# A dense squared-ReLU layer: block 0 starts its first matmuls on half the columns, with the other transposes in between

## Chip, cores, metric

One core of a Trainium2 chip. The metric is the device time of one launch in microseconds, as a median of runs. The program runs on one core, so a run has no second die to be compared with; every run quoted here was fast (within 1.5% of the fastest run of the same kernel). A profile is one execution, taken with the hardware profiler; its span is about 1.8 us shorter than the device time of the same run (290.3 against 292.11 us for the kernel before).

## The reference

```python
# x (1, 2048, 576)  w1 (576, 4608)  b1 (4608)  w2 (4608, 576)  b2 (576), all bf16
h = jnp.einsum("bsd,df->bsf", x, w1) + b1
r = jnp.where(h > 0, h, 0)
out = jnp.einsum("bsf,fd->bsd", r * r, w2) + b2
```

## The kernel before

The 2048 rows are worked on in four blocks of 512. For each block, TensorE (PE) first multiplies with w1 to get the hidden values, ScalarE (ACT) adds the bias and clips, VectorE (DVE) squares, and PE multiplies with w2. Both products contract over the partitions, so x is needed transposed. Blocks 1 to 3 get it by a transposing DMA during block 0. Block 0 cannot wait for that: it loads four row tiles of x (128 rows each) and transposes them on PE, 20 transposes of 128x128, whose results in PSUM are copied to SBUF by DVE and ACT.

The first product of block 0 (`a_full`) makes four groups of 128 hidden columns, over 4 x 128 + 64 rows of w1: the 128-row steps use `w1n`, k = 0 to 3, and the last 64 rows are the "half-row" matmuls on `w1n8`. The other 32 groups follow in `a_rows`, from `w1_h`.

```python
WARM = [512] * 6 + [256]              # matmuls on constants until x lands
...
load_x(nc.sync, 0)
load_x(nc.scalar, 1)
load_x(nc.sync, 2)
load_x(nc.scalar, 3)
for k in range(NK):                   # NK = 4
    load_w1n(nc.sync, k)              # 128 rows x 512 columns of w1 each
... # b1 and w1n8 on the GpSimd queue; w1_h, then the rest, on the sync queue
for j in range(RT):                   # RT = 4 row tiles of block 0
    cols = slice(j * P, (j + 1) * P)
    ta = ps_h.tile([P, 3, P], BF16, name="ta", tag="ph")
    for i in range(3):
        keep(nc.tensor.transpose(ta[:, i, :], xs[:, j, i * P:(i + 1) * P], ident[:]))
    keep(nc.vector.tensor_copy(out=xT0[:, O:O + 3, cols], in_=ta[:, :, :]))
    tb = ps_o.tile([P, 2, P], BF16, name="tb", tag="po")
    keep(nc.tensor.transpose(tb[:, 0, :], xs[:, j, 3 * P:4 * P], ident[:]))
    keep(nc.tensor.transpose(tb[:, 1, :], xs[:, j, D - P:D], ident[:]))
    keep(nc.scalar.copy(out=xT0[:, O + 3, cols], in_=tb[:, 0, :]))
    keep(nc.scalar.copy(out=xT0[:, E3, cols], in_=tb[:, 1, :]))
dup_windows(0)                        # two DVE copies that shift 64 partitions
... # in a_full(0, "k_outer"):
for k in range(NK):
    for g in range(G):                # G = 4 groups, one PSUM bank each, 512 columns
        full(g, k, k == 0, False)     # banks[g] += w1n[:, k, g].T @ xT[:, O + k, :]
    if k == 1:
        make_b1T()                    # one transpose of the bias, one copy
for i in (1, 0):
    pair(i, False, True)              # the half-row matmuls on w1n8
    ...
```

## Time and profile before

| | before |
|---|---|
| device time, median (first 3 runs, and one more with the result) | 292.98 us (292.62 to 293.26); 292.8 of four |
| span of the profiled run | 290.3 us (device time 292.11) |
| PE busy | 285.7 us, 98% |
| first matmul on w1n / first half-row matmul | 5.71 / 9.31 us |

Rows of the profile's page (busy time and share; then the span in 40 slices, in tenths):

```profile
PE 285.7 (98%) x2409; PEld 178.0 (61%) x2412; DVE 81.5 (28%) x189; ACT 94.2 (32%) x154; POOL 2.7 (1%) x10
...
PE   8999999999999999999999999999999999999995
...
PEclk9999999999999999999999999999999999999999
```

PE is the limit everywhere but in the first and last slice. The change works inside the first 10 us, so only the timeline of PE there counts. Columns: start, duration, engine, source line, operation, output and input, count, and in brackets the idle time ahead of it with what ended it.

```profile
0.78 2.93 PE L61 MATMUL wps<-const-bfloat16-1.0 128*128 128x512 bf16 x7 [0.78 <-PEq L306]
3.51 0.52 PE L138 MATMUL ta<-ident,x_sb 128*128 128x128 bf16 x3
...
4.47 0.25 PE L142 MATMUL tb<-ident,x_sb 128*128 128x128 bf16 x1
4.56 0.33 PE L138 MATMUL ta<-ident,x_sb 128*128 128x128 bf16 x3
...
5.06 0.22 PE L142 MATMUL tb<-ident,x_sb 128*128 128x128 bf16 x1
5.71 1.89 PE L194 MATMUL pn<-xTw,w1n 128*128 128x512 bf16 x8 [0.43 <-ACT xTw L143]
7.43 0.22 PE L151 MATMUL b1T_ps<-ident,b_rows 128*128 128x128 bf16 x1
7.49 1.89 PE L194 MATMUL pn<-xTw,w1n 128*128 128x512 bf16 x8
9.31 0.39 PE L188 MATMUL pn<-xTw,w1n_89 64*128 64x512 bf16 x1
```

Read the starts: matmuls are pipelined, so the durations overlap. Ten transposes start between 3.51 and 4.56 (107 ns apart, only the last step is 86), ten more between 4.56 and 5.12 (56 ns apart). Then PE has nothing to issue until 5.71, which is the hole that the change aims at: the last of the four row tiles has to be copied out of PSUM before the first 512-column matmul. The drop from 107 to 56 ns is the array's clock, which the row PEclk and the clock column of the windows view do not show:

```profile
0.00:3.46 3.46, 2.68 (x7) 0.87 (x7) 0.00 (x0) 1.49 (x2) 2.75 (x10) 1.00 0.45 134
3.46:5.71 2.25, 1.82 (x23) 1.68 (x21) 1.31 (x4) 1.39 (x8) 0.00 (x0) 1.00 1.01 302
```

(Columns: window, its length, busy time and count of PE, weight loads, DVE, ACT, GpSimd, then granted clock, DMA share, GB/s.) The clock column says 1.00 in a window whose seven warm-up matmuls (6 of 512 columns, one of 256) take 2.93 us, about 0.43 us per 512 columns, twice the 216 ns of the same size later on. The trace's record of the clock simply begins at 4.52 us; before it there is no record and the view counts that as full speed. The DMA share of 1.01 says that all 16 engines are full while these loads land. The page's lines of those loads (size, then microseconds from issue to landing, as a median of the group):

```profile
w1n<-in_w_dram SPq DMA_DIRECT2D x4, 128.0 KB, 4.0
x_sb<-in_x_dram ACTq DMA_DIRECT2D x2, 144.0 KB, 3.0
x_sb<-in_x_dram SPq DMA_DIRECT2D x2, 144.0 KB, 2.8
```

### The profile page before, as it was taken

The page shows a single profiled execution, that of the slowest core. Times are in us where ns is not written, and L with a number is a line of the kernel's source. Part 1 is how long each engine was busy: PE and PEld are TensorE (multiplying, and loading weights), DVE is VectorE, ACT ScalarE, POOL GpSimd, SP SyncE. Part 2 cuts the span into 40 slices and gives each one's busy share as a digit, 9 for nine tenths or more (in the row PEclk, how much of TensorE's full clock was granted, in tenths as well). Part 3 has the DMA queues.
Part 4 walks back from the last instruction along what each step waited for, and adds up shares of the span by engine and source line. Part 5 has one row for each costly group of instructions (what it writes and reads, how often), then busy time and mean ns, then how long its engine had stood idle before and what let it go on. Part 6 is the DMA issues. An engine that isn't in the chain of part 4 may idle for free.

```text
span 290.3 us, 5455 instructions
## 1 busy us (share of the span) xinstructions
PE 285.7 (98%) x2409; PEld 178.0 (61%) x2412; DVE 81.5 (28%) x189; ACT 94.2 (32%) x154; POOL 2.7 (1%) x10
## 2 busy tenths in 40 slices
PE   8999999999999999999999999999999999999995
PEld 4444444444677777777744444444447777777774
DVE  3344544444531011110025444444440111100111
ACT  4566666666400000000027666666670000000000
POOL 3000000000000000000000000000000000000000
PEclk9999999999999999999999999999999999999999
DMA  7999999900000000000000000000000000000000
GB/s 203 214 212 177 255 357 265 164 1 2 0 23 0 23 20 20 23 3 20 20 23 0 3 0 2 0 2 0 2 0 2 20 24 20 21 2 23 20 20 24
DMA packets 27096, 16.05 MB, mean 55 GB/s; under 512 B 11028, under 2 KB 27040, under 8 KB 27072
## 3 DMA queue, kind: packets, MB, share of 16 engines
q1 hardware_dynamic: 26688, 15.32, 23.9%
q8 instruction: 19, 0.31, 0.4%
q10 hardware_dynamic: 288, 0.30, 0.3%
q0 software_dynamic: 96, 0.07, 0.1%
q14 instruction: 5, 0.04, 0.0%
HBM read 11.36 MB, written 2.36 MB: 47 GB/s over the span
## 4 chain that ended last, share of the span: by engine, by line
PE 98%; ACT 0%; issue 0%; DVE 0%
PE po L233 49%; PE ph L173 42%; PE pn L194 5%; PE wps L61 1%; PE ph L175 1%; PE pn L188 1%; PE ta L138 0%; ACT xTw L143 0%; DVE o_sb L242 0%; ACT xTw L144 0%; PE tb L141 0%; PE tb L142 0%; PE b1T_ps L151 0%; PE pn L190 0%
## 5 line engine op out<-in xcount | busy, mean ns | idle before, releaser
L233 PE MATMUL po<-w_sb,hT 128*128 128x288 bf16 x1152 | 141.4, 286 | 0.0
L233 PEld LDWEIGHTS <-hT 128*128 128x128 bf16 x1152 | 112.7, 98 | 28.8
L173 PE MATMUL ph<-xTw,w_h 64*128 64x512 bf16 x576 | 124.6, 376 | 0.0
L175 PE MATMUL ph<-xTw,w_h 64*128 64x512 bf16 x576 | 124.6, 376 | 0.0
L173 PEld LDWEIGHTS <-w_h 64*128 64x128 bf16 x576 | 54.1, 94 | 68.3
L161 ACT ACTIVATE r<-ph,b1T 128x512 bf16<-128x512 f32 x128 | 81.1, 685 | 41.6 <-PE ph L175 41.6
L162 DVE TENSOR_TENSOR hT<-r 128x512 bf16<-128x512 bf16 x144 | 61.2, 426 | 77.3 <-ACT r L161 76.7
L175 PEld LDWEIGHTS <-w_h 64*128 64x128 bf16 x576 | 54.1, 94 | 0.0
L242 DVE TENSOR_TENSOR o_sb<-po,b_bc 128x288 bf16<-128x288 f32 x32 | 13.3, 453 | 123.9 <-PE po L233 123.9
L161 ACT ACTIVATE r<-pn,b1T 128x512 bf16<-128x512 f32 x16 | 10.3, 688 | 78.8 <-PE pn L190 77.5
L194 PE MATMUL pn<-xTw,w1n 128*128 128x512 bf16 x61 | 14.0, 379 | 0.8 <-ACT xTw L143 0.4
L194 PEld LDWEIGHTS <-w1n 128*128 128x128 bf16 x64 | 6.0, 98 | 8.0 <-issue 1.4
L61 PE MATMUL wps<-const-bfloat16-1.0 128*128 128x512 bf16 (+1 forms) x7 | 2.9, 594 | 0.8 <-PEq L306 0.8
L113 DVE COPY xTw<-xTw 64x2048 bf16<-64x2048 bf16 x4 | 2.8, 690 | 0.4 <-ACT xTw L144 0.3
L114 DVE COPY xTw<-xTw 64x2048 bf16<-64x2048 bf16 x4 | 2.7, 687 | 0.1
L139 DVE COPY xTw<-ta 128x384 bf16<-128x384 bf16 x4 | 1.3, 358 | 4.2 <-PE ta L138 4.2
L188 PE MATMUL pn<-xTw,w1n_89 64*128 64x512 bf16 x8 | 2.4, 379 | 0.0
L190 PE MATMUL pn<-xTw,w1n_89 64*128 64x512 bf16 x8 | 2.4, 379 | 0.0
L61 PEld LDWEIGHTS <-const-bfloat16-1.0 128*128 128x128 bf16 x7 | 0.9, 135 | 2.1 <-issue 2.1
L98 ACT ACT_TABLE_LOAD x1 | 1.3, 1283 | 1.7 <-PEq L306 1.7
L138 PE MATMUL ta<-ident,x_sb 128*128 128x128 bf16 x12 | 1.6, 265 | 0.0
L143 ACT COPY xTw<-tb 128x128 bf16<-128x128 bf16 x4 | 1.1, 282 | 1.2 <-PE tb L142 1.1
(21 smaller groups left out, 10.2 us busy)
## 6 DMA issues: line engine op xcount, KB each, us to landing
w_sb<-in_w_dram SPq DMA_DIRECT2D x6, 864.0 KB, 11.4
w_h<-in_w_dram SPq DMA_DIRECT2D x14, 288.0 KB, 7.4
out_dram<-o_sb SPq DMA_DIRECT2D x15, 144.0 KB, 1.8
w_h<-in_w_dram SPq DMA_DIRECT2D x4, 144.0 KB, 4.1
w1n<-in_w_dram SPq DMA_DIRECT2D x4, 128.0 KB, 4.0
x_sb<-in_x_dram ACTq DMA_DIRECT2D x2, 144.0 KB, 3.0
x_sb<-in_x_dram SPq DMA_DIRECT2D x2, 144.0 KB, 2.8
b_bc<-in_b_dram SPq DMA_DIRECT2D x1, 144.0 KB, 7.6
```

The source lines that it names most:

```text
L61: keep(nc.tensor.matmul(wps[:, 0:n], lhsT=ones[:, 0:P], rhs=ones[:, 0:n], start=True, stop=True))
L113: keep(nc.vector.tensor_copy(out=xT[0:H, SPC:SPC + 4, :], in_=xT[H:P, E3:E3 + 4, :]))
L114: keep(nc.vector.tensor_copy(out=xT[H:P, SPC:SPC + 4, :], in_=xT[0:H, O:O + 4, :]))
L161: keep(nc.scalar.activation(out=r[:], in_=bank[:], func=ACT.Relu, bias=b1T[:, ft:ft + 1], scale=1.0))
L162: keep(nc.vector.tensor_tensor(out=hTs[sb][:, ft, :], in0=r[:], in1=r[:], op=ALU.mult))
L173: keep(nc.tensor.matmul(bx[:], lhsT=w1_h[0:H, LO_C[i], jc], rhs=xT[0:H, LO_W[i], :], start=(i == 0), stop=(i == NC - 1)))
L175: keep(nc.tensor.matmul(by[:], lhsT=w1_h[H:P, UP_C[i], jc], rhs=xT[H:P, UP_W[i], :], start=(i == 0), stop=(i == NC - 1)))
L188: keep(nc.tensor.matmul(banks[2 * i][:], lhsT=w1n8[0:H, i, :], rhs=xT[0:H, SPC, :], start=start, stop=stop))
L190: keep(nc.tensor.matmul(banks[2 * i + 1][:], lhsT=w1n8[H:P, i, :], rhs=xT[H:P, E3, :], start=start, stop=stop))
L194: keep(nc.tensor.matmul(banks[g][:], lhsT=w1n[:, k, g * P:(g + 1) * P], rhs=xT[:, O + k, :], start=start, stop=stop))
L233: keep(nc.tensor.matmul(po[h][:, 0:DH], lhsT=hT[:, ft, jj * P:(jj + 1) * P], rhs=w2_sb[:, ft, h * DH:(h + 1) * DH], start=(i == 0), stop=( ...
L242: keep(nc.vector.tensor_tensor(out=o_sb[:, h * DH:(h + 1) * DH], in0=po[h][:, 0:DH], in1=b2_bc[:, h * DH:(h + 1) * DH], op=ALU.add,))
```

## The change

The intent: don't hold the first matmuls until all four row tiles are transposed and copied. Once tiles 0 and 1 are there, multiply for their 256 columns, and put the transposes of tiles 2 and 3 between those matmuls. The loads are rearranged: x tiles 1 to 3 all go on the ACT queue, so that w1n starts one issue earlier on the sync (SP) queue. The diff, cut to its core:

```diff
-    load_x(nc.scalar, 1)
-    load_x(nc.sync, 2)
-    load_x(nc.scalar, 3)
+    for rt in range(1, RT):
+        load_x(nc.scalar, rt)
...
+    def x_copies(h):                       # half h: 256 columns
+        hc = slice(h * HS, (h + 1) * HS)
+        for k in range(NK):
+            src = half_banks[h][k][:, 0, :]
+            if k % 2 == 0:
+                keep(nc.vector.tensor_copy(out=xT0[:, O + k, hc], in_=src))
+            else:
+                keep(nc.scalar.copy(out=xT0[:, O + k, hc], in_=src))
+        keep(nc.vector.tensor_copy(out=xT0[:, E3, hc], in_=half_banks[h][NK - 1][:, 1, :]))
...
-                for k in range(NK):
-                    for g in range(G):
-                        full(g, k, k == 0, False)
-                    if k == 1:
-                        make_b1T()
+                def part(h, k):
+                    hc = slice(h * HS, (h + 1) * HS)
+                    for g in range(G):
+                        keep(nc.tensor.matmul(banks[g][:, hc], lhsT=w1n[:, k, g * P:(g + 1) * P],
+                                              rhs=xT[:, O + k, hc], start=(h == 0 and k == 0), stop=False,
+                                              skip_group_check=True))
+                x_transposes(0)
+                x_transposes(1)
+                x_copies(0)
+                part(0, 0)
+                part(0, 1)
+                x_transposes(2)
+                part(0, 2)
+                x_transposes(3)
+                x_copies(1)
+                dup_windows(0)
+                part(0, 3)
+                part(1, 0)
+                make_b1T()
+                for k in range(1, NK):
+                    part(1, k)
```

Each `part(h, k)` is four matmuls of 256 columns. Only `part(0, 0)` has the start flag; the second half of a bank is first written without it.

More of the change, by code (lines that the diff above doesn't have):

```diff
@@ L133, with x_transposes @@
     xT0 = xT_blk[0]
-    for j in range(RT):
-        cols = slice(j * P, (j + 1) * P)
-        ta = ps_h.tile([P, 3, P], BF16, name="ta", tag="ph")
-        for i in range(3):
-            keep(nc.tensor.transpose(ta[:, i, :], xs[:, j, i * P:(i + 1) * P], ident[:]))
-        keep(nc.vector.tensor_copy(out=xT0[:, O:O + 3, cols], in_=ta[:, :, :]))
-        tb = ps_o.tile([P, 2, P], BF16, name="tb", tag="po")
-        keep(nc.tensor.transpose(tb[:, 0, :], xs[:, j, 3 * P:4 * P], ident[:]))
-        keep(nc.tensor.transpose(tb[:, 1, :], xs[:, j, D - P:D], ident[:]))
-        keep(nc.scalar.copy(out=xT0[:, O + 3, cols], in_=tb[:, 0, :]))
-        keep(nc.scalar.copy(out=xT0[:, E3, cols], in_=tb[:, 1, :]))
-    dup_windows(0)
+    HS = SB // 2
+    tb_po = [ps_o.tile([P, 2, HS], BF16, name="tb", tag="po") for _ in range(2)]
+    tb_ph = [ps_h.tile([P, 2, HS], BF16, name="tb", tag="ph") for _ in range(4)]
+    half_banks = [tb_ph, None]
+    def x_transposes(j):
+        h, q = divmod(j, 2)
+        qc = slice(q * P, (q + 1) * P)
+        for k in range(NK + 1):
+            bank, slot, c0 = (half_banks[h][k], 0, k * P) if k < NK else (half_banks[h][NK - 1], 1, D - P)
+            keep(nc.tensor.transpose(bank[:, slot, qc], xs[:, j, c0:c0 + P], ident[:]))
+    def x_copies(h):
[7 more added lines that the diff above has]
+        keep(nc.vector.tensor_copy(out=xT0[:, E3, hc], in_=half_banks[h][NK - 1][:, 1, :]))
     b1T = const.tile([P, NFT], FP32, name="b1T")
@@ L188, in pair @@
             keep(nc.tensor.matmul(banks[2 * i][:], lhsT=w1n8[0:H, i, :], rhs=xT[0:H, SPC, :],
-                             start=start, stop=stop))
+                             start=start, stop=stop, skip_group_check=order == "k_outer"))
             keep(nc.tensor.matmul(banks[2 * i + 1][:], lhsT=w1n8[H:P, i, :], rhs=xT[H:P, E3, :],
-                             start=start, stop=stop))
+                             start=start, stop=stop, skip_group_check=order == "k_outer"))
         def full(g, k, start, stop):
@@ L205, in a_full @@
             if order == "k_outer":
-                for k in range(NK):
+                tb_new = [ps_h.tile([P, 2, HS], BF16, name="tb", tag="ph") for _ in range(2)]
+                half_banks[1] = tb_new + tb_po
+                def part(h, k):
+                    hc = slice(h * HS, (h + 1) * HS)
                     for g in range(G):
-                        full(g, k, k == 0, False)
-                    if k == 1:
-                        make_b1T()
+                        keep(nc.tensor.matmul(banks[g][:, hc], lhsT=w1n[:, k, g * P:(g + 1) * P],
[16 more added lines that the diff above has]
+                    part(1, k)
             else:
```

## The prediction

> **What bounds the kernel now.** TensorE. The page's busy table gives PE 98% of a 290.3 us span; the chain that ended last is 98% PE at a granted clock of 1.00. The change touches only the first 10 us, which the timeline shows:
>
> - 0.78-3.71 us: warm-up matmuls
> - 3.51-5.12: 20 transposes of x, the first ten 107 ns apart, the rest 56 ns
> - 5.12-5.71: the only real hole. PE waits for the last copies ("0.43, ACT xTw"; the last DVE copy also ends at 5.57)
> - 5.71-9.31: 16 matmuls of 512 columns, 216 ns apart, and the bias transpose (0.06)
> - 9.31: half-row matmuls; 9.75: the w1_h stage
>
> So at most about 0.6 us of 293 (0.2%) can be won. All of it is on the critical path.
>
> **What the change does.**
> - 32 matmuls of 256 columns replace 16 of 512. I estimate 109 ns each: the Trainium skill, "TensorE: Matmul & The Clock Gate", section "Wait — 56ns, not 53.3ns?", has N/2.4 GHz plus about 2.5 ns, which fits this trace's 216 and 56 ns. Total 3.49 us against 3.46: no cost. Weight loads double, but 98 ns hide behind 109.
> - Only half the copies stand before the first matmul. The copy of k=0 can start at about 4.35 us. From 358 ns for 384 elements and 200 ns for 36 I estimate 0.30 us for 256, so the first matmul starts at 4.7-4.8, after an idle of 0.15-0.2 instead of 0.6.
> - w1n's loads go out one issue (0.45 us) earlier on SP; x tile 3 goes out 0.45 later on ACT.
>
> **What gives part of it back.** The w1n loads land at about 4.95, 6.0, 6.7 and 7.2 us (issue plus time to landing), 0.6 to 1.2 us before use. The DMA engines are full there (share 1.01 in 3.46-5.71), and the same bytes, x tile 3 included, go ahead of k=1, so it lands perhaps at 5.3-5.9. PE will want k=1 at about 5.2. I expect a wait of 0.1-0.6 us there, perhaps small ones for k=2 and 3. The hole becomes a wait for weights.
>
> Second half: its copies hide behind part(0,3). The window copies (0.69 us each) start at about 8.1 instead of 5.9 and end at 9.5; the bias copy follows at 9.7. The half-row matmuls need only the first (8.8), the upper rows of w1_h the second at about 10.3. No stall.
>
> **Sum.** Without waits for weights the half-row matmuls would start at 8.85 instead of 9.31. With them I expect 9.15: a gain of 0.15 us. If k=1 lands no earlier than before, it's 0.3 us worse. Later stages shift unchanged: w1_h loads land about a microsecond before use.
>
> **Predicted: 292.8 us, 292.3 to 293.3** (the three runs before spread over 0.64 us). Faster by over 2%: 0.5%; within 2%: 99%; slower by over 2%: 0.5%.
>
> **What the profile would show.** First w1n matmul at 4.7-4.9 us; 256-column matmuls 109 ns apart; PE or weight-load idle before k=1 of 0.1-0.6 us (DMA or "issue"); half-row matmuls from 8.85-9.5; ACT's first bias activation at 9.5-10.0; later stages equal to within 0.1 us in sum.
>
> **What would make it wrong.** 256-column matmuls paced by weight loads[...]. The clock not yet at full speed, or falling back in the new waits. w1_h stalling a PE that arrives sooner. Correctness: only the first matmul into each bank has the start flag, and the second half's first overwrites still-clear columns; I expect a correct result.

## The result

| | before | after |
|---|---|---|
| median, first comparison (4 runs each) | 292.8 us | 292.38 us (292.1 to 292.61) |
| ratio, 95% interval | | 0.9983 (0.9966 to 1.0000) |
| ratio, repeated (6 runs against 11) | | 1.0001 (0.9988 to 1.0013) |
| ratio of the kernel before to itself (5 against 11) | 0.9992 (0.9981 to 1.0004) | |
| span of the profiled run | 290.3 us | 290.8 us |
| first matmul on w1n / first half-row matmul | 5.71 / 9.31 us | 4.74 / 9.73 us |

A ratio is the mean time of one kernel's fast runs over that of the other's fast runs of the same rounds, so it is not quite the ratio of the medians. The result is correct. The time is the same: the interval of the first comparison touches 1, the repetition sits on 1, and two sets of runs of the kernel before differ by half as much as the first comparison. The profiles even disagree in sign with the first comparison: the profiled run of the changed kernel is 0.4 us *longer*. Both facts need an explanation, and a difference of 0.1% needs care.

The timeline of PE in the changed kernel, to be held against the one above:

```profile
0.79 2.93 PE L61 MATMUL wps<-const-bfloat16-1.0 128*128 128x512 bf16 x7 [0.79 <-PEq L335]
3.51 1.27 PE L143 MATMUL tb<-ident,x_sb 128*128 128x128 bf16 x10
4.74 0.60 PE L221 MATMUL pn<-xTw,w1n 128*128 128x256 bf16 x4
5.95 0.61 PE L221 MATMUL pn<-xTw,w1n 128*128 128x256 bf16 x4 [0.62 <-DMA w1n<-in_w_dram]
6.40 0.44 PE L143 MATMUL tb<-ident,x_sb 128*128 128x128 bf16 x5
6.68 0.60 PE L221 MATMUL pn<-xTw,w1n 128*128 128x256 bf16 x4
7.12 0.44 PE L143 MATMUL tb<-ident,x_sb 128*128 128x128 bf16 x5
7.39 1.04 PE L221 MATMUL pn<-xTw,w1n 128*128 128x256 bf16 x8
...
8.32 1.47 PE L221 MATMUL pn<-xTw,w1n 128*128 128x256 bf16 x12
9.73 0.39 PE L197 MATMUL pn<-xTw,w1n_89 64*128 64x512 bf16 x1
```

The hole ahead of the first matmul has shrunk as intended: that matmul starts at 4.74 us, a microsecond earlier. Then the second group of four, `part(0, 1)`, stands still until 5.95. (The bracket's 0.62 us counts from the modelled end of the matmul before. By the starts, four matmuls at 109 ns from 4.74 are through at 5.18, so PE is idle for 0.77 us.) From there on nothing waits: it is 3.78 us to the half-row matmuls. The chain of waits (start, length, what) says what it waited for and what the rest is made of:

```profile
1.65 4.26 DMA w1n<-in_w_dram
5.91 0.05 issue
5.95 0.61 PE pn L221 x4
6.56 0.28 PE tb L143 x5
...
8.49 1.31 PE pn L221 x12
```

The load of w1n k=1, issued at 1.65 us, took 4.26 us to land. In the kernel before the same load was issued at 2.11 and landed at 6.03; nobody noticed, since PE wanted it only at 6.57. So issuing it 0.46 us earlier brought it in 0.12 us earlier, while PE wanted it 1.4 us earlier. The last line also gives the matmul rate: 1.31/12 = 109 ns per 256 columns. The loads as a group:

```profile
w1n<-in_w_dram SPq DMA_DIRECT2D x4, 128.0 KB, 4.3
x_sb<-in_x_dram ACTq DMA_DIRECT2D x3, 144.0 KB, 3.2
```

Everything after the half-row matmuls is unchanged: 290.34 - 9.31 = 281.03 us before, 290.77 - 9.73 = 281.04 us after. This stretch takes 281.02 to 281.06 us in 13 of the 14 profiles of this document (all but a_bal_w8sp), so the start of the half-row matmuls tells a profile's whole time. The late window copies and the bias copy on DVE end at 10.07 us without holding PE:

```profile
9.15 0.69 DVE L113 COPY xTw<-xTw 64x2048 bf16<-64x2048 bf16 x1
9.87 0.20 DVE L161 CAST b1T<-b1T_ps 128x36 f32<-128x36 bf16 x1
```

### The profile page after: what moved, and what is told of

Read it like the earlier page. It is cut to its first block, busy times and chain, and to the rows that moved or that the text cites. A ratio compares the mean times of both kernels' runs of the same rounds, so it can differ in the third digit from the quotient of the medians.

```text
span 290.8 us, 5486 instructions
## 1 busy us (share of the span) xinstructions
PE 286.3 (98%) x2428; PEld 179.6 (62%) x2428; DVE 81.7 (28%) x191; ACT 93.9 (32%) x150; POOL 2.7 (1%) x10
## 4 chain that ended last, share of the span: by engine, by line
PE 97%; DMA 1%; SPq 0%; DVE 0%; issue 0%
PE po L262 49%; PE ph L182 42%; PE pn L203 4%; DMA w1n<-in_w_dram 1%; PE pn L221 1%; PE ph L184 1%; PE pn L197 1%; PE tb L143 0%; DVE o_sb L271 0%; SPq L73 0%; SPq L70 0%; PE b1T_ps L160 0%; PE pn L199 0%
## 5 line engine op out<-in xcount | busy, mean ns | idle before, releaser
L203 PE MATMUL pn<-xTw,w1n 128*128 128x512 bf16 x48 | 10.9, 379 | 0.0
L203 PEld LDWEIGHTS <-w1n 128*128 128x128 bf16 x48 | 4.5, 98 | 5.9 <-issue 0.8
L221 PE MATMUL pn<-xTw,w1n 128*128 128x256 bf16 x32 | 4.2, 273 | 0.6 <-DMA w1n<-in_w_dram 0.6
L221 PEld LDWEIGHTS <-w1n 128*128 128x128 bf16 x32 | 3.0, 99 | 1.3 <-DMA w1n<-in_w_dram 0.9
L150 DVE COPY xTw<-tb 128x256 bf16<-128x256 bf16 x4 | 1.0, 289 | 6.2 <-PE tb L143 6.2
L152 ACT COPY xTw<-tb 128x256 bf16<-128x256 bf16 x4 | 1.3, 374 | 3.1 <-PE tb L143 3.1
```

The lines of the kernel that those rows point to most:

```text
L203: keep(nc.tensor.matmul(banks[g][:], lhsT=w1n[:, k, g * P:(g + 1) * P], rhs=xT[:, O + k, :], start=start, stop=stop))
L221: keep(nc.tensor.matmul(banks[g][:, hc], lhsT=w1n[:, k, g * P:(g + 1) * P], rhs=xT[:, O + k, hc], start=(h == 0 and k == 0), stop=False, s ...
```

## The experiments

Two questions. First, where did the gain of the split go? **Theory W**: into the wait for w1n k=1. Rival: the smaller matmuls, the interleaving or the late copies cost it. Second, why do runs of one kernel differ by more than this change? **Theory A**: the moment at which TensorE's clock rises to full speed differs from run to run. **Theory B**: only the landing of loads differs. Twelve kernels ran in three batches; the kernels of a batch shared a chip and its runs of the kernel before.

### b_again: the kernel before, again

No edit.

> The kernel before, again, as its own control. Ratio 1.000 within 0.002 if chips and runs agree. In the two profiles taken so far the half-row matmuls start at 9.31 us (before) and 9.73 us (changed), so the change looks 0.42 us slower there, while the timed runs say 0.4 us faster. Theory A (clock phase): the moment at which TensorE reaches full speed differs from run to run; the profile of before caught an early one (4.5 us). Then another profile of the same kernel can show transposes 107 ns apart beyond 4.5 us, or first matmuls 427 ns apart, and half-row matmuls up to 1 us later. Theory B (landing): the clock rises at the same time in every run and only the landing of loads varies; then the transposes again become fast at 4.4-4.6 us and only waits move.

Measured: 292.39 us median, ratio 0.9992 (0.9981 to 1.0004). In its profile (PE timeline):

```profile
4.57 0.53 PE L138 MATMUL ta<-ident,x_sb 128*128 128x128 bf16 x3
...
5.10 0.38 PE L138 MATMUL ta<-ident,x_sb 128*128 128x128 bf16 x3
...
6.03 1.89 PE L194 MATMUL pn<-xTw,w1n 128*128 128x512 bf16 x8 [0.43 <-ACT xTw L143]
...
9.63 0.39 PE L188 MATMUL pn<-xTw,w1n 64*128 64x512 bf16 x1
```

The third row tile's five transposes, which took 0.28 us in the first profile (4.56 to 4.84), take 0.53 us here (4.57 to 5.10), and the trace's clock record begins at 5.20 us, not 4.52. The half-row matmuls come 0.32 us later: 0.32/0.68 = 0.47 us per microsecond that the clock is late, about the half that a half-speed clock should cost. Theory A holds in two profiles of one kernel, and B is not needed for this difference: w1n k=0 landed later here too (5.64 us against 4.94), but PE waited for the copies until 6.03 anyway. The span is 0.3 us longer (290.7). So the first profile of before had caught an early clock. Its run (292.11 us) was also 0.69 us faster than the median of the timed runs (292.8).

### a_again: the changed kernel, again

No edit.

> The changed kernel again. Ratio 0.9983 again (0.997 to 1.000). A wait for w1n k=1 again, until 5.7-6.1 us, half-row matmuls at 9.5-9.8. If theory A holds, a late clock costs this kernel less, since PE waits for k=1 anyway: its profile and its runs spread less than those of before.

Measured: 292.6 us median (292.16 to 293.11), ratio 1.0001 (0.9988 to 1.0013), just outside the expected 0.997 to 1.000. PE timeline:

```profile
4.74 1.01 PE L221 MATMUL pn<-xTw,w1n 128*128 128x256 bf16 x4
6.10 0.61 PE L221 MATMUL pn<-xTw,w1n 128*128 128x256 bf16 x4 [0.36 <-DMA w1n<-in_w_dram]
...
9.98 0.39 PE L197 MATMUL pn<-xTw,w1n 64*128 64x512 bf16 x1
```

The clock record begins at 5.65 us here, so the first four matmuls took 1.01 us in place of 0.60, and this was free: they ran inside the wait for k=1, which landed at 6.06. The wait is there a second time. The expected smaller spread is not: these runs have a standard deviation of 0.41 us, those of b_again 0.14. That part of the expectation failed; with five or six runs I don't read more into it. The half-row start of 9.98 misses the expected 9.5 to 9.8: after the wait for k=1 came a second one of 0.1 us, for k=2, which landed at 6.88 us here and at 6.43 in the first profile.

### b_newloads: the order of the loads alone

```diff
-    load_x(nc.scalar, 1)
-    load_x(nc.sync, 2)
-    load_x(nc.scalar, 3)
+    for rt in range(1, RT):
+        load_x(nc.scalar, rt)
```

> Before, with only the order of the loads changed (x tiles 1 to 3 on ACT, w1n one issue earlier). x tile 3 landed at 4.4 us before and 6.15 in the changed kernel. Here all four row tiles stand before the first matmul, so a late tile 3 stops everything: I expect the first matmul at 6.5-7.0 instead of 5.7 and 0.7-1.3 us more than before (ratio 1.002 to 1.005). If the load order is harmless, ratio 1.000.

Measured: 293.39 us median (292.87 to 295.11), ratio 1.0041 (1.0017 to 1.0065). Its timeline waits 0.17 us for x tile 3 (until 5.36), the first matmul starts at 6.41 (just under the 6.5 expected), and the clock was late as well: all 20 transposes are about 107 ns apart. So the first matmul is 0.70 us later than in the first profile of before, but the wait for tile 3 is at most 0.17 us of that and a later first transpose (3.67 us, not 3.51) another 0.16; the rest, about 0.4 us, is the clock. By the timed runs the new load order is no gain by itself. That the late tile 3 is the cause of their loss is not shown. Two of the six runs took about 295 us; they were not profiled, and why is open.

### a_oldloads: the new compute order with the old loads

```diff
-    for rt in range(1, RT):
-        load_x(nc.scalar, rt)
+    load_x(nc.scalar, 1)
+    load_x(nc.sync, 2)
+    load_x(nc.scalar, 3)
```

> The changed compute order with the loads of before. w1n k=1 goes out at 2.1 us instead of 1.65 but x tile 3 no longer shares the engines with it. If k=1's landing is set by bytes ahead of it, it lands at 5.9-6.0 as in both profiles, and the time is that of the changed kernel within 0.15 us. If the issue time sets it, it lands 0.45 us later (6.3) and the time rises by 0.4 us.

Measured: 292.79 us median (292.49 to 294.37), ratio 1.0020 (1.0001 to 1.0040), half-row matmuls at 9.77 us with a clock that rose at 4.33. k=1 landed at 5.94 us, issued at 2.15; in a_again it was issued at 1.67 and landed at 6.06. So the earlier issue did not bring the last piece sooner in this pair (more profiles are compared below). But here k=0 is late too (5.31 us), so PE waits 0.72 us ahead of the first matmul and 0.30 us of weight-load idle remains ahead of the second group. Issuing w1n first was needed for the first matmul, and did little for the second.

### a_k0only: the wait taken away

```diff
-   keep(nc.tensor.matmul(banks[g][:, hc], lhsT=w1n[:, k, g * P:(g + 1) * P],
+   keep(nc.tensor.matmul(banks[g][:, hc], lhsT=w1n[:, 0, g * P:(g + 1) * P],
```

> The changed kernel with its wait for weights taken away: block 0's first stage multiplies with w1n k=0 at every k, so no matmul waits for k=1 to 3 (wrong result on purpose; all loads still run). Theory W (the gain of the split goes into waiting for w1n k=1, whose last piece lands at 5.9-6.1 us): the half-row matmuls start at 8.8-9.3, depending on when the clock rises (4.3 to 6.5 us), against 9.73 and 9.98 in the two profiles of the changed kernel, and the time is 0.4-0.9 us under it (ratio to before 0.997-0.999). Rival: 256-column matmuls, interleaved transposes or late copies cost the gain; then the half-row matmuls still start at 9.6 or later.

Measured: wrong as intended (relative error 0.07), 292.3 us median (292.12 to 292.48), ratio 0.9983 (0.9966 to 1.0000). PE timeline:

```profile
4.73 1.77 PE L221 MATMUL pn<-xTw,w1n 128*128 128x256 bf16 x8
6.33 0.44 PE L143 MATMUL tb<-ident,x_sb 128*128 128x128 bf16 x5
...
9.66 0.39 PE L197 MATMUL pn<-xTw,w1n 64*128 64x512 bf16 x1
```

No wait is left, and yet the half-row matmuls start at 9.66, which by the letter of the expectation speaks for the rival. Even so it is earlier than in both profiles of the changed kernel (9.73 and 9.98), and the clock was later here, which cannot have helped. How much later, the matmuls show: the first eight matmuls take 1.60 us from start to start of what follows. With c of them at 213 ns (half clock) and the rest at 109, 213c + 109(8 - c) = 1600 gives c = 7, so the clock rose at about 6.2 us (this trace has no clock record). Corrected with the 0.47 us per microsecond of b_again, an estimate, this kernel would have started its half-row matmuls at 9.66 - 0.47 x (6.2 - 4.76) = 8.98 with the clock of the changed kernel's first profile, where they started at 9.73; and at 9.66 - 0.47 x (6.2 - 5.65) = 9.40 with that of a_again, where they started at 9.98. So the wait for weights costs 0.6 to 0.75 us at those clocks, and it costs less the later the clock rises. Counting without the slope gives nearly the same: eight gaps of 109 ns are 0.87 us, 0.73 less than 1.60, and 9.66 - 0.73 = 8.93. Before's still earlier clock (4.52) would hardly help, since PE is idle from 4.57 to 4.73 anyway: about 8.95, against 9.31 measured for before, so the split without waits would gain about 0.35 us. The timed runs do not confirm this: their ratio of 0.9983 is the one that the changed kernel had in its first comparison, and its interval (0.9966 to 1.0000) nearly reaches a_again's 1.0001.

### a_long and b_long: weights landed and clock up, in both kernels

```diff
-    WARM = [512] * 6 + [256]
+    WARM = [512] * 24
```

> The changed kernel with 24 warm-up matmuls of 512 columns: the transposes start after 7.6 us, when all these loads have landed and the clock is up. That takes both the wait for weights and the clock out of the comparison with b_long; the total is longer for both. From the first transpose to the first half-row matmul I expect 4.8-4.95 us (20 transposes of 56 ns, 32 matmuls of 109, bias 0.06, one hole of 0.15-0.25), 0.35-0.45 us less than b_long. If 256-column matmuls or interleaving cost something, the two differ by under 0.2 us.

> The kernel before with the same 24 warm-up matmuls. From the first transpose to the first half-row matmul 5.2-5.4 us (1.12 of transposes, a hole of 0.6-0.75 for the copies, 3.52 of matmuls). Total about 4 to 5.5 us over the kernel before.

Measured: 296.19 us (ratio to before 1.0122) and 296.8 us (1.0140). a_long's PE timeline:

```profile
8.29 0.72 PE L143 MATMUL tb<-ident,x_sb 128*128 128x128 bf16 x10
9.17 1.03 PE L221 MATMUL pn<-xTw,w1n 128*128 128x256 bf16 x8 [0.16 <-DMA w_h<-in_w_dram]
...
13.37 0.39 PE L197 MATMUL pn<-xTw,w1n 64*128 64x512 bf16 x1
```

and b_long's:

```profile
8.50 0.33 PE L138 MATMUL ta<-ident,x_sb 128*128 128x128 bf16 x3
...
10.21 1.89 PE L194 MATMUL pn<-xTw,w1n 128*128 128x512 bf16 x8 [0.43 <-ACT xTw L144]
...
13.81 0.39 PE L188 MATMUL pn<-xTw,w1n 64*128 64x512 bf16 x1
```

From first transpose to first half-row matmul: 13.81 - 8.50 = 5.31 us before, 13.37 - 8.29 = 5.08 us changed. So the split gains 0.23 us when nothing else interferes (one profile of each), less than the 0.35 to 0.45 that I expected. The timed medians differ by 0.61 us in the same direction. Ahead of the first transpose the two profiles differ by another 0.21 us, and there the clock is the cause: it rose at 5.45 us in a_long and at 5.88 in b_long, so 0.21/0.43 = 0.49 us per microsecond, on the same warm-up matmuls, which wait for no load. This is theory A once more. The hole of before is 0.59 us (9.62 to 10.21), just under the 0.6 to 0.75 expected; the changed kernel's is 0.32 (8.85 to 9.17), not 0.15 to 0.25. At full clock the rest of tile 1's transposes covers only 4 x 56 ns of the copy of k=0, at half clock 4 x 107. (The release named in the bracket, a load of w1_h, is not one that this matmul waits for; the copy of k=0 had ended just before.) Splitting the matmuls costs next to nothing: 32 at 109 ns for 16 at 216. The rival, that small matmuls or interleaving eat the gain, falls.

### a_tr2early: fill the wait

```diff
                 part(0, 0)
-                part(0, 1)
                 x_transposes(2)
+                part(0, 1)
                 part(0, 2)
```

> The changed kernel with row tile 2 transposed before part(0,1), not after it, so that this work falls into the wait for w1n k=1. Theory W: k=1's last piece still lands at 5.9-6.1 us, part(0,1) starts then, and the half-row matmuls follow 0.28 us sooner after it: 3.5 us after the start of part(0,1) in place of 3.78, at 9.4-9.7. Time 0.2-0.3 us under the changed kernel, if k=2 and x tile 3 don't stop it instead. Rival (the clock alone decides): no shift beyond what the clock's moment explains.

Measured: 292.5 us median (291.8 to 293.54), ratio 1.0000 (0.9983 to 1.0016); half-row matmuls at 8.99 us, span 290.0. From the start of part(0,1) at 5.49 to there it is 3.50 us, as expected (this much follows from moving 0.28 us of transposes ahead of it). But this profile is a lucky one on both counts: its clock record begins at 3.80 us, and k=1's last piece landed at 5.37. The chain of waits shows a wait of another kind in its place:

```profile
4.24 0.66 ACT xTw L152 x2
4.90 0.02 issue
4.92 0.30 DVE xTw L153
5.22 0.04 issue
5.27 0.38 PE tb L143 x4
```

Tile 2's second transpose writes the PSUM bank out of which the two last copies of tiles 0 and 1 (ACT, then DVE) are still being read, until 5.22. So the version is limited at once by the next thing in line. The timed runs do not separate it from before.

### a_balanced and a_bal_w8sp: loads in the order of use

```diff
     load_x(nc.sync, 0)
-    for rt in range(1, RT):
-        load_x(nc.scalar, rt)
-    for k in range(NK):
-        load_w1n(nc.sync, k)
+    load_x(nc.scalar, 1)
+    load_w1n(nc.sync, 0)
+    load_w1n(nc.scalar, 1)
+    load_x(nc.sync, 2)
+    load_x(nc.scalar, 3)
+    load_w1n(nc.sync, 2)
+    load_w1n(nc.scalar, 3)
```

a_bal_w8sp also moves the two loads of w1n8 from the GpSimd queue to the sync queue, after w1n k=2.

> The changed compute order with loads in the order of use, alternating on two queues: SP x0, w1n0, x2, w1n2; ACT x1, w1n1, x3, w1n3. k=1 is then issued at 1.2 us with 426 KB ahead of it or beside it, not 720 KB. Theory W: k=1 lands at 4.4-5.0, PE waits under 0.2 us for it, half-row matmuls at 8.9-9.3, ratio to before 0.997-0.9985: faster than both kernels. If stragglers among the 16 engines set the landing whatever the order, k=1 still lands after 5.5 and nothing is won (ratio 0.999-1.001).

> As a_balanced, and the two w1n8 loads go from the POOL queue to SP after w1n2, so that they no longer compete with x and w1n from 2.2 us. If they made the stragglers, k=2 and k=3 land earlier too and the half-row matmuls start up to 0.2 us earlier than in a_balanced; else the same within 0.1 us.

Measured: a_balanced 293.28 us, ratio 1.0007 (0.9988 to 1.0027), half-row matmuls at 10.64; a_bal_w8sp 293.33 us, ratio 1.0020 (1.0003 to 1.0037), half-row matmuls at 9.91. Both expectations failed. In a_balanced the wait for k=1 is gone, but the first transposes started later (3.90 us, not 3.51, waiting for x), x tile 2 landed at 6.57 and w1n k=2 at 7.53, and PE waited for each of them; the engines were full, and what came sooner for one load came later for others. In a_bal_w8sp k=2 landed at 6.80 us, and the only wait left for w1n is 0.1 us for it; the half-row matmuls start 0.73 us before those of a_balanced, more than the 0.2 expected, though its clock was later (6.46 us against 5.82). But the w1_h loads now go out at 5.14 us in place of 3.57: weight loads wait twice 0.3 us for w1_h, and the stretch after the half-row matmuls is 0.9 us longer than in all other profiles. The rest of that 0.9 us stays unexplained.

### b_warm2: fewer warm-up matmuls

```diff
-    WARM = [512] * 6 + [256]
+    WARM = [512] * 2
```

> The kernel before with two warm-up matmuls instead of seven: PE is then idle from about 1.7 to 3.5 us and the clock should rise later. Theory A (the spread of the runs and of the profiles is the moment the clock rises): all 20 transposes 107 ns apart, the first matmuls 427 ns apart until 6.9 us or later, half-row matmuls 0.9 to 2.5 us after 9.31, ratio 1.003-1.008. If warm-up matmuls don't matter: ratio 1.000.

Measured: 293.62 us median (293.07 to 294.21), ratio 1.0028 (1.0010 to 1.0046), just under the 1.003 expected; the clock record begins at 7.46 us, all transposes are 107 ns apart, half-row matmuls at 10.38, 1.07 us after the first profile. As expected by theory A: the clock's moment alone moves this kernel by a microsecond. (For a clock 2.94 us later this is less than 0.47 us per microsecond, since PE is idle for 0.59 us of that time, whatever the clock.)

### a_trfirst: a version meant to beat both

```diff
+    load_x(nc.scalar, 1); load_x(nc.sync, 2); load_x(nc.scalar, 3)    # loads of before
                 x_transposes(0)
                 x_transposes(1)
                 x_copies(0)
+                x_transposes(2, range(3))
+                x_transposes(3, range(3))
                 part(0, 0)
-                part(0, 1); x_transposes(2); part(0, 2); x_transposes(3)
+                x_transposes(2, range(3, 5))
+                x_transposes(3, range(3, 5))
                 x_copies(1)
                 dup_windows(0)
-                part(0, 3)
                 part(1, 0)
+                part(0, 1)
+                part(1, 1)
                 make_b1T()
-                for k in range(1, NK):
+                for k in range(2, NK):
+                    part(0, k)
                     part(1, k)
```

(Abridged: lines are joined, and the changed loads stand in one line. The second half's PSUM tiles also take the free banks first.)

> A version meant to beat both: loads of before; all transposes ahead of the matmuls but for the last two columns of tiles 2 and 3, which follow part(0,0); then k by k, both halves of each, so that the weights are wanted as late as possible (k=1 at about 6.0, k=2 at 7.0). Expected: first matmul at 5.0-5.7 (as w1n k=0 lands), no wait for k=1 over 0.3 us, half-row matmuls at 8.9 with a clock that rises at 4.5 and 9.4 with one at 5.6 us; 0.2-0.4 us under the kernel before at the same clock, ratio 0.998-0.9995.

Measured: correct, 292.17 us median (291.56 to 292.64), ratio 0.9987 (0.9973 to 1.0000): the lowest ratio of the correct kernels besides the first comparison of the change itself, and not proved. Its profile was not lucky: w1n k=0 landed at 5.90 us and stopped the first matmul.

```profile
5.94 0.61 PE L222 MATMUL pn<-xTw,w1n 128*128 128x256 bf16 x4 [0.54 <-DMA w1n<-in_w_dram]
```

After that no wait is left until the half-row matmuls at 9.82, but the expected 8.9 to 9.4 are missed by the late k=0.

### What the landing of a load looks like inside

A load is done when its last of 16 pieces is. From the trace's landing records (each piece has its time), for the load that mattered; us from the span's start:

```
profile      load  issued  9th piece     15th   last
before       k=1   2.11    5.32          5.95   6.03
after        k=1   1.65    4.72          5.41   5.91
a_again      k=1   1.67    4.85          5.22   6.06
b_newloads   k=1   1.66    4.71          4.89   4.96
a_tr2early   k=1   1.66    4.80          5.20   5.37
before       k=0   1.65    4.59          4.90   4.94
a_trfirst    k=0   1.67    4.59          5.61   5.90
```

From before to after, the middle piece of k=1 came 0.6 us earlier and the last one only 0.12. The last piece is 0.25 to 1.3 us behind the middle one. The same records exist for six profiles of each order of loads. In the new order (after, a_again, b_newloads, a_k0only, a_tr2early, a_long) k=1 landed between 4.96 and 6.32 us, 5.75 on average; in the old one (before, b_again, a_oldloads, b_warm2, a_trfirst, b_long) between 5.86 and 6.33, 6.06 on average. So issuing k=1 0.46 us earlier brought it 0.3 us on average, within a spread of 1.4. For k=0 the gain is clear: 4.09 to 4.31 us in the new order, 4.94 to 5.94 in the old. The profile of before had the earliest of those, 4.94; in the other five k=0 landed at 5.30 or later, close to or after the 5.71 at which that profile started its first matmul. I have not found what delays single pieces; the records do not say on which engine a piece came.

## Why the prediction was right

The call (292.8 us, range 292.3 to 293.3, same within 2%) holds: 292.38, near the lower end. The time alone says little, though, and its hit is in part luck: the range is 1.0 us wide, more than the spread of the first runs (0.64 us), so a change without any effect would have hit it too, and the forecast gain of 0.15 us is too small for these runs to show. The spans of the timed runs, less 281.03 us, give an estimate of where the half-row matmuls start on average: 9.70 us for before (11 runs) against 9.75 for the changed kernel (6 runs of the same batch; 9.57 in its first four). So neither before's 9.31 nor the predicted 9.15 is typical.

- **"At most about 0.6 us can be won", at the hole ahead of the first w1n matmul.** Right. The hole measures 0.59 us in before, in b_again and in b_long.
- **109 ns per 256 columns, no cost of the split.** Right: 1.31 us for 12. The Trainium skill ("TensorE: Matmul & The Clock Gate", "Wait — 56ns, not 53.3ns?") gave the formula, and this trace agrees at 128, 256 and 512 columns (56, 109, 216 ns).
- **First matmul at 4.7 to 4.8.** Right: 4.74. The reason is narrower than I wrote: the hole is 0.15 us only since the transposes ahead of it run at half clock. At full clock it is 0.32 (a_long).
- **"The hole becomes a wait for weights": 0.1 to 0.6 us ahead of k=1, landing at 5.3 to 5.9.** The mechanism is right: both profiles of the changed kernel show the wait. That it costs 0.6 to 0.75 us of the total rests on a_k0only with a clock correction, which is an estimate. The term of the sum that was mis-sized is this wait, since k=1 landed later than estimated in both profiles: at 5.91 and 6.06, with PE idle 0.77 us in the first profile (5.18 to 5.95; 5.18 is 4.74 plus four times 109 ns). I had estimated the landing from the bytes ahead of it; the middle piece came well before that estimate (4.7 to 4.9 us) and the last of the 16, which decides, at its end or past it. The Trainium skill says as much ("DMA: Bandwidth & Descriptors", "Why a DMA increments its semaphore by 16 and not by 1": the engines finish independently and the semaphore counts them); the runs add that the last can be 1.3 us behind.
- **Half-row matmuls at 9.15 (8.85 to 9.5), ACT's first bias activation at 9.5 to 10.0.** Missed in the profile by the same term: 9.73, and 10.17. My own "if k=1 lands no earlier than before, it's 0.3 us worse" is the case that happened in the two profiles.
- **Second half hidden; late stages unchanged.** Right: no wait ahead of part(1,0) or after, and 281.03 against 281.04 us for the rest.
- **What I left out: the clock as a term of the noise.** I read the clock column's 1.00 as "full speed throughout", took the rise at 4.5 us as a fixed fact and listed "not yet at full speed" only as a danger. It lies anywhere from 3.80 to 6.46 us in these profiles with seven warm-up matmuls, worth about 0.47 us per microsecond while PE has work. The Trainium skill says that the window is free-running ("TensorE: Matmul & The Clock Gate", "What's actually happening"), and the runs agree in that the rise is not tied to the first matmul, which starts at 0.78 or 0.79 us in all of them. The clock is not what made one profile of each kernel say "0.42 us slower": 4.52 against 4.76 us is worth at most 0.11 us of it, and the rest is the wait for k=1, which outweighs the smaller hole. But before's profile was a fast run, 0.69 us under the median of its timed runs, with an early clock and an early k=0, and the changed kernel's was 0.15 us over its own; hence the "0.4 us faster" of the first timed rounds beside it. Neither figure is the effect of the change. Whether the clock or the landings make most of the spread of the timed runs is not shown. A late clock also hides inside the wait for k=1, as a_again's first four matmuls show.

What stays open: what delays single pieces of a load; the two runs of 295 us in b_newloads; how much of the spread of the timed runs is the clock and how much the landings; whether the timed runs gain what the estimate from a_k0only promises; and the true effect of the change within about 0.15%, which these runs cannot resolve.

## What to carry to other kernels

When you bring forward the first use of a buffer, look at when each of its loads lands, piece by piece, and not only at the wait that you remove: here w1n k=1 landed 0.5 us ahead of its use before the change, and 0.7 us later than it was wanted after it. In a_balanced, with the DMA engines full, reordering the loads moved the wait rather than removing it. Ordering the work so that each load is wanted as late as possible is an idea that a_trfirst tried, at a ratio of 0.9987 that is not proved. And before reading a difference of a few tenths of a microsecond from two profiles, profile one kernel twice: TensorE's clock alone moved before's half-row matmuls by 0.32 us.

## What the Trainium skill lacked or had wrong

- "TensorE: Matmul & The Clock Gate", "Back-to-back issue gap", gives 81 ns (128 columns) and 131 ns (512) per matmul for a stream of weight load and matmul pairs, and calls N/2.4 + 2.5 the isolated gap that over- or under-counts. In this case every matmul has its own weight load, and the streams ran at 56, 109 and 216 ns for 128, 256 and 512 columns: the formula, not the sustained figures.
- The same page, "What's actually happening", advises not to fit a cold count since the ramp is under 1% of a span. That holds (a microsecond of late clock cost about 0.47 of 290 us), but it lacks the consequence: the moment of the rise, 3.80 to 6.46 us here with the first matmul always at 0.78 or 0.79, is worth over 1 us at 0.47 us per microsecond, more than a change of 0.1 to 0.2%. The ±500 ns that the section gives for the moment of the rise is too narrow here: it moved over 2.66 us. (Its other remark, that the number of cold matmuls differs from run to run, fits.)
- "DMA: Bandwidth & Descriptors", "Why a DMA increments its semaphore by 16 and not by 1", says that the 16 engines finish independently and gives no size. Here the last piece of the 128 KB loads in the table was 0.25 to 1.3 us behind the middle (9th) piece.
- No page says that a profile's clock can read 1.00 for lack of a record: the windows view here says 1.00 while matmuls of 512 columns run at 0.43 us each, against 0.216 later.
